# Spectral mixing behind a short convolution: Y brought into its second layout by TensorE transposes, the convolution taps loaded to one partition on another queue than the first x unit, and a reordered seam

## The chip, the cores and the metric

One core of one Trainium2 chip. The metric is the device time of one execution in microseconds (us); lower is better. The kernel before takes 183.05 us (median of 3 runs, 183.0 to 183.22). Ratios below are the mean time of one kernel's fast runs over that of the kernel before in the same rounds, so they are not quite the ratio of the medians that stand beside them. In the profile lines PE is TensorE's matmuls, PEld its weight loads, DVE VectorE, ACT ScalarE and POOL GpSimd; the granted clock is the share of its full clock that TensorE ran at. Instants in the text are us from the start of the span, which is 1.7 to 1.9 us shorter than the time in most executions.

## The reference, cut to what matters

```python
# x: (8, 3264, 192), weight: (8, 7)
w = softmax(weight)                       # taps, per head of 24 channels
x = causal 7-tap convolution of x with w  # along the sequence
X = rfft(x, axis=1)                       # only 64 modes are kept
Y[m] = X[m] @ (w_r[m] + 1j * w_i[m])      # 64 complex 192x192 matrices: 18.9 MB
y = irfft(Y, n=3264)
u = x + y
out = u + relu(u @ w_ch)                  # float32, 20 MB
```

## The kernel before

The kernel has a loading part (x, then the weights of the 64 modes in 16 groups, all through GpSimd's software queue, "the stream", cast to bf16 on the way), a seam from the last weights to the steady loop, and an output loop over 108 units. The parts that the change touches:

```python
# the start: taps broadcast to 128 partitions, then the first x unit, both on the sync queue
wraw = sp.tile([P, H, KK], F32, tag="wraw")
nc.sync.dma_start(out=wraw[:]..., in_=bass.AP(tensor=weight.tensor, ..., ap=[[0, P], [1, H * KK]]))
x32 = sp.tile([P, 8, D], F32, tag="x32")
nc.sync.dma_start(out=x32[:], in_=...)          # 1024 rows of 768 B
load_unit(0, 2)                                 # the software queue ("the stream") begins
...                                             # softmax of the taps on all 128 partitions

# two mode groups of the mix -> 128 rows of Y; a transfer makes the layout [mode rows, batch, channel]
def mix(g):
    ...
    nc.scalar.activation(out=ymix[:], in_=zt[:, 0:D], func=ACT.Copy, scale=...)
    nc.sync.dma_start(out=zy[16 * i:16 * i + 16, :, :], in_=ymix[:, :])   # 8 of these
def mix_t(g, ymix):                             # and the transposed copy yeT, by TensorE
    ...

# the seam, after the last weights
zw_part(0); zw_part(1)                          # 16 products yeT x w_ch into four banks, then copies
for n in range(4): gz(n)                        # four units were prefilled; gz = product with Z, relu
prefill(); gy(0); gz(4); gy(1); prefill(); gy(2); gz(5); gy(3)    # gy = product with Y, add, store
```

Of the kernel before, what the change touches and what calls it, by code (L numbers as in the profile page):

```python
# [9 lines left out]
ALU = mybir.AluOpType  # L10
ACT = mybir.ActivationFunctionType
AX = mybir.AxisListType
F32 = mybir.dt.float32
BF16 = mybir.dt.bfloat16
# [4 lines left out]
def kernel(  # L19
# [9 lines left out]
    nc = tc.nc  # L29
    B, S, D = x.shape  # L30
    H, KK = weight.shape
    MODES = moe_w_r.shape[0]
# [3 lines left out]
    P = 128  # L36
# [36 lines left out]
    def load_last():  # L73
# [8 lines left out]
    ident = constp.tile([P, P], BF16, tag="ident")  # L82
# [12 lines left out]

    setup_stack = ExitStack()
    sp = setup_stack.enter_context(tc.tile_pool(name="setup", bufs=1))
    wraw = sp.tile([P, H, KK], F32, tag="wraw")
    nc.sync.dma_start(out=wraw[:].rearrange("p h k -> p (h k)"),
                      in_=bass.AP(tensor=weight.tensor, offset=weight.offset, ap=[[0, P], [1, H * KK]]))  # L100

    x32 = sp.tile([P, 8, D], F32, tag="x32")
    nc.sync.dma_start(out=x32[:], in_=bass.AP(tensor=x.tensor, offset=x.offset + (WIN * 10 - OV) * D,
                                              ap=[[D, P], [WIN * D, 8], [1, D]]))
# [18 lines left out]
    win0 = constp.tile([P, D], BF16, tag="win0")  # L123
    win1 = constp.tile([P, D], BF16, tag="win1")
    wB0 = constp.tile([P, D], BF16, tag="wB0")
    for b in range(1, B):
# [9 lines left out]
        elif b == 4:  # L136
            nc.gpsimd.dma_start(out=wB0[0:64, :], in_=moe_w_ch[P:D, :])
            load_last()

    nc.vector.memset(cband[:], 0.0)  # L140

    NB = 32 + OV
# [2 lines left out]
    for g in range(4):  # L145
        i0 = OV if g == 0 else 0
        nc.vector.tensor_copy(out=diagc[32 * g:32 * g + 32, i0:NB],
                              in_=diag[32 * g:32 * g + 32, 32 * g - OV + i0:32 * g + 32])
    nc.vector.tensor_scalar(out=ident[:], in0=diag[:], scalar1=0.0, scalar2=None, op0=ALU.is_equal)

    halfpi = sp.tile([P, 1], F32, tag="halfpi")
# [4 lines left out]
    def make_k(u):  # L156
# [2 lines left out]
                                in0=sidx[:, w0:w0 + n].unsqueeze(2).to_broadcast([P, n, MODES]),  # L159
                                in1=midx[:, :].unsqueeze(1).to_broadcast([P, n, MODES]), op=ALU.mult)  # L160

    wmax = sp.tile([P, H], F32, tag="wmax")
    nc.vector.reduce_max(out=wmax[:], in_=wraw[:], axis=AX.X)
    wsub = sp.tile([P, H, KK], F32, tag="wsub")
    nc.vector.tensor_tensor(out=wsub[:], in0=wraw[:],
                            in1=wmax[:, :].unsqueeze(2).to_broadcast([P, H, KK]), op=ALU.subtract)
    wexp = sp.tile([P, H, KK], F32, tag="wexp")
    nc.scalar.activation(out=wexp[:], in_=wsub[:], func=ACT.Exp)
    nc.scalar.copy(out=x_all[:, 0, 10:18, :], in_=x32[:])
    wsum = sp.tile([P, H], F32, tag="wsum")  # L170
    nc.vector.reduce_sum(out=wsum[:], in_=wexp[:], axis=AX.X)
    nc.vector.tensor_scalar(out=wsum[:], in0=wsum[:], scalar1=1e-9, scalar2=None, op0=ALU.add)
    wrec = sp.tile([P, H], F32, tag="wrec")
    nc.vector.reciprocal(out=wrec[:], in_=wsum[:])
    wsb = sp.tile([P, H, KK], F32, tag="wsb")
    nc.vector.tensor_tensor(out=wsb[:], in0=wexp[:],
                            in1=wrec[:, :].unsqueeze(2).to_broadcast([P, H, KK]), op=ALU.mult)

    ps1 = ExitStack()
    pconv = ps1.enter_context(tc.tile_pool(name="pconv", bufs=3, space=PSUM))  # L180
    pxx = ps1.enter_context(tc.tile_pool(name="pxx", bufs=1, space=PSUM))



# [2 lines left out]
    for k in range(KK):  # L187
        nc.vector.scalar_tensor_tensor(out=scaled[:, k, :, :],
                                       in0=diagc[:, :].unsqueeze(1).to_broadcast([P, H, NB]), scalar=float(k),
                                       in1=wsb[:, :, k:k + 1].to_broadcast([P, H, NB]),  # L190
                                       op0=ALU.is_equal, op1=ALU.mult)
        for o in bps:
            nc.tensor.matmul(o[:, 0:H * NB], ident[:], scaled[:, k, :, :].rearrange("p h i -> p (h i)"),
                             start=(k == 0), stop=(k == KK - 1))
# [41 lines left out]
    yeT = constp.tile([P, 2, 2 * MODES * B], BF16, tag="yeT")  # L236
# [65 lines left out]
    dq = []  # L302
    xq = []

    nc.scalar.activation(out=wmax[:, 0:1], in_=halfpi[:], func=ACT.Sin)
    ascale = constp.tile([P, 1], F32, tag="ascale")

    zy = constp.tile([P, B, D], BF16, tag="zy")
# [54 lines left out]
    pt = ctx.enter_context(tc.tile_pool(name="pt", bufs=4, space=PSUM))  # L363
# [28 lines left out]
    for p in range(4):  # L392
        k = 0
        for i in range(11):
            n = 8 if i < 4 else 7
# [47 lines left out]


    mixed = [None]

    def mix(g):
        i, half = divmod(g, 2)
        if half == 0:
            mixed[0] = py.tile([P, 512], F32, tag="y", name="yp")  # L450
        zt = mixed[0]
        for j in range(3):
            for pos in range(4):
                nc.tensor.matmul(zt[32 * pos:32 * pos + 32, 0:D],  # L454
                                 xt[:, j, half:half + 2, :, MG * i + pos].rearrange("p s k -> p (s k)"),
                                 wtiles[g][:, pos, j, :], start=(half == 0 and j == 0),
                                 stop=(half == 1 and j == 2), tile_position=(0, 32 * pos),
                                 skip_group_check=True)
        if half == 0:
            return None  # L460

        ymix = workp.tile([P, D], BF16, tag="ymix")
        nc.scalar.activation(out=ymix[:], in_=zt[:, 0:D], func=ACT.Copy,  # L463
                             scale=ascale[:, 0:1] if i == 0 else 2.0 / S)
        nc.sync.dma_start(out=zy[16 * i:16 * i + 16, :, :], in_=ymix[:, :])
        return ymix

    def mix_t(g, ymix):
        zt = mixed[0]
# [9 lines left out]
    zwi = {}  # L479
    zwps = []  # L480

    def zw_part(h):
        for k in range(2):
            zp = zwps[2 * h + k]
            for i in range(2):
                b = 4 * h + 2 * k + i
                for e, wn in ((0, win0), (1, win1)):
                    nc.tensor.matmul(zp[:, D * i:D * i + D], yeT[:, e, b:2 * MODES * B:B], wn[:, :],  # L488
                                     start=(e == 0), stop=(e == 1), skip_group_check=True)
            zt = zwip.tile([P, 2 * D], BF16, tag=f"zw{h}{k}", name="zw")  # L490
            if h == 0:
                nc.vector.tensor_copy(out=zt[:, 0:D], in_=zp[:, 0:D])
                nc.scalar.copy(out=zt[:, D:2 * D], in_=zp[:, D:2 * D])
            else:
                nc.vector.tensor_copy(out=zt[:], in_=zp[:, 0:2 * D])
            b = 4 * h + 2 * k
            zwi[(h, 0, k)] = zt[:]
            zwi[(h, 1, k)] = zy[:, b:b + 2, :].rearrange("p b e -> p (b e)")

    def g_full(u, zp, part):  # L500
        h, w, k = u
# [39 lines left out]
    def relu(zp):  # L541
        return nc.scalar.activation(out=zp[:, 0:2 * D], in_=zp[:, 0:2 * D], func=ACT.Relu)  # L542
# [50 lines left out]

    ahead(0)
    gq = [0, 1]
    TPER = (1, 2, 1, 2, 2, 2, 1, 1, 2, 1, 2, 1, 2, 1, 1)
    zps = []

    def bank(n):
# [6 lines left out]
    def prefill():  # L606
        zps.append(bank(len(zps)))
        ab_full(seq[len(zps) - 1], zps[-1])
# [6 lines left out]
    for g in range(NGRP):  # L615
        last = g == NGRP - 1
        m = mix(g)
        if g == 6:
            wts0_stack.close()
            cTb = ctx.enter_context(tc.tile_pool(name="stashb", bufs=1)).tile([P, CTW], BF16, tag="cTb")  # L620
            nc.vector.memset(cTb[:, NSLOT * WIN:CTW], 0.0)
            cTs[3] = cTb[:, :]
        if g in (0, 1, 2):
            load_weights(g + 7, wp)
        elif 7 <= g and g + 4 < NGRP:
            load_weights(g + 4, None if g == 10 else wp)
        if not last:
            for _ in range(TPER[g]):
                t_next(2 if g < 6 else 3)
            if gq:  # L630
                g_part(gq.pop(0))
            if g == 2:
                load_weights(10, None)

            if g in (11, 13, 14):
                prefill()
        else:
            keep_warm(4)
        if m is not None:
            mix_t(g, m)  # L640
        if g == NGRP - 2:
            zwps += [pt.tile([P, 512], F32, tag="p", name="zwps") for _ in range(3)]
            prefill()
            keep_warm(6)
    zwps.append(py.tile([P, 512], F32, tag="y", name="zwps"))
# [7 lines left out]
    zwip = ctx.enter_context(tc.tile_pool(name="zwip", bufs=1, side="right"))  # L653


    def gz(n):
        g_full(seq[n], zps[n], 0)
        relu(zps[n])

    def gy(n):  # L660
        g_full(seq[n], zps[n], 1)
        finish_unit(seq[n], zps[n])

    zw_part(0)
    zw_part(1)
    for n in range(4):
        gz(n)
    prefill()
    gy(0)
    gz(4)  # L670
    gy(1)
    prefill()
    gy(2)
    gz(5)
    gy(3)
    N, NF = len(seq), 6
    zword, yword = {}, {}
    for j in range(NF, N + 6):
        o0, o1 = [], []
        if j < N:  # L680
            zps.append(bank(j))
            o0 = z_ops(seq[j], zps[j], 0)
        if NF <= j - 2 < N:
            o1 = z_ops(seq[j - 2], zps[j - 2], 1)
        zword[j] = run_pair(o0, o1, zword.get(j - 2))
        if NF <= j - 2 < N:
            relu(zps[j - 2])
        elif j - 2 < NF:
            gy(j - 2)
        o0, o1 = [], []  # L690
        if NF <= j - 4 < N:
            o0 = y_ops(seq[j - 4], zps[j - 4], 0)
        if NF <= j - 5 < N:
            o1 = y_ops(seq[j - 5], zps[j - 5], 1)
        yword[j - 4] = run_pair(o0, o1, yword.get(j - 5))
        if NF <= j - 5 < N:
            finish_unit(seq[j - 5], zps[j - 5])
# [29 lines left out]
```

## Time and profile before

| | before |
|---|---|
| time | 183.05 us |
| stream's first packets | 5.6 us |
| last mix (last weights landed) | 109.36 us |
| first half-height matmul with Y (the loop is under way) | 117.77 us |
| first of the last four adds (VectorE; start) | 174.68 us |
| end of the span | 181.4 us |

Read it as stretches: loading, which ends with the last mix; the seam, to the loop's first half-height Y matmul; and the loop. The lines themselves are shown in the prediction.

### The profile page before, as it was taken

The numbers are of one execution on the slowest core, as the hardware profiler recorded it, in microseconds if no ns is written. First come the engines' busy times: TensorE is split into PE (matmuls) and PEld (weight loads), VectorE is DVE, ScalarE is ACT, GpSimd is POOL, SyncE is SP. The second block draws the span as 40 slices with busy tenths as digits, with TensorE's granted clock in tenths as the row PEclk, the third lists the DMA queues.
The fourth block names the chain that finished last, engine by engine and source line by source line (L and its number), as shares of the span: only waits on it lengthen the run. The fifth ranks groups of instructions, "written<-read, shape, count | busy, mean of one in ns | idle before, by whom it ended". The sixth has DMA issues, their size and how long they took to land.

```text
span 181.4 us, 5402 instructions
## 1 busy us (share of the span) xinstructions
PE 147.8 (81%) x2115; PEld 128.9 (71%) x2115; DVE 127.8 (70%) x256; ACT 112.9 (62%) x189; POOL 48.8 (27%) x74
## 2 busy tenths in 40 slices
PE   0373579989889969894649977999999999999970
PEld 0242359978779959783538866699999999999940
DVE  5879986553544446974462554679999999999990
ACT  2353994555558617774444453588888888888850
POOL 7969332459322244432523100000000000000000
PEclk9999558999999999999985999999999999999997
DMA  2999999999999999999999990479999999999995
GB/s 60 247 191 191 192 192 191 193 190 192 193 192 193 204 206 207 206 208 210 203 206 207 207 178 11 150 238 306 345 358 353 349 324 366 348 341 328 326 353 188
DMA packets 66819, 42.37 MB, mean 234 GB/s; under 512 B 30218, under 2 KB 66794, under 8 KB 66794
## 3 DMA queue, kind: packets, MB, share of 16 engines
q0 software_dynamic: 36048, 19.75, 78.2%
q1 hardware_dynamic: 30746, 22.28, 37.5%
q8 instruction: 16, 0.26, 0.7%
q14 instruction: 9, 0.07, 0.1%
HBM read 40.31 MB, written 21.01 MB: 338 GB/s over the span
## 4 chain that ended last, share of the span: by engine, by line
DMA 54%; PE 38%; POOL 2%; issue 2%; DVE 1%; DVEq 0%; ACT 0%; POOLq 0%; ACTq 0%
DMA x_all<-in_x_dram 29%; PE z L520 19%; DMA wt<-in_moe_w_i_dram 19%; PE z L537 13%; DMA fst<-in_moe_w_i_dram 6%; PE tp L418 2%; POOL x_all L61 2%; PE z L502 1%; PE yp L454 1%; PE zwps L488 1%; DVE t L572 1%; PE z L510 0%; POOL wt L251 0%; DVEq L722 0%; ACT ymix L463 0%
## 5 line engine op out<-in xcount | busy, mean ns | idle before, releaser
L572 DVE TENSOR_TENSOR t<-z,x_all 128x384 f32<-128x384 f32 x108 | 59.4, 557 | 3.9 <-PE z L537 1.5
L542 ACT ACTIVATE z<-z 128x384 f32<-128x384 f32 x108 | 50.7, 476 | 11.6 <-PE z L520 1.7
L537 PE MATMUL z<-zy,gst 64*128 64x384 bf16 x204 | 46.1, 323 | 0.2
L520 PE MATMUL z<-zw,gst 64*128 64x384 bf16 x204 | 46.1, 323 | 0.0
L520 PE MATMUL z<-win,cTa 64*128 64x192 bf16 x375 | 40.9, 243 | 0.0
L267 ACT CAST x_all<-cp 122x864 bf16<-122x864 f32 (+2 forms) x34 | 28.7, 880 | 15.4 <-PE cp L260 15.2
L520 PEld LDWEIGHTS <-cTa 64*128 64x128 bf16 x450 | 34.9, 94 | 2.8
L260 PE MATMUL cp<-x_all,cband 128*128 128x192 bf16 (+2 forms) x192 | 25.9, 287 | 8.8 <-DVE x_all L269 4.6
L260 PEld LDWEIGHTS <-cband 128*128 128x128 bf16 x192 | 19.7, 109 | 12.7 <-issue 5.4
L61 POOL DMA_DIRECT2D x_all<-in_x_dram x23 | 22.0, 969 | 10.8 <-DMA x_all<-in_x_dram 8.5
L269 DVE CAST x_all<-cp 122x768 bf16<-122x768 f32 (+2 forms) x14 | 14.7, 1054 | 13.2 <-PE cp L260 13.2
L423 ACT COPY cTa<-tp 128x854 bf16<-128x854 bf16 (+1 forms) x16 | 14.1, 910 | 14.7 <-PE tp L418 14.7
L282 PE MATMUL xp<-x_all,fst 122*128 122x192 bf16 (+1 forms) x216 | 22.0, 251 | 0.9 <-DVE x_all L269 0.5
L282 PEld LDWEIGHTS <-fst 122*128 122x128 bf16 (+1 forms) x216 | 18.2, 99 | 2.1 <-DVE x_all L269 0.7
L520 PEld LDWEIGHTS <-gst 64*128 64x128 bf16 x204 | 18.9, 94 | 0.7 <-issue 0.7
L520 PE MATMUL z<-win,cTb 64*128 64x192 bf16 x135 | 19.2, 243 | 0.0
L422 DVE COPY cTa<-tp 128x854 bf16<-128x854 bf16 (+1 forms) x17 | 10.6, 623 | 10.8 <-PE tp L418 10.6
L520 PE MATMUL z<-wB,cTa 64*128 64x192 bf16 x75 | 18.2, 243 | 0.0
L537 PEld LDWEIGHTS <-gst 64*128 64x128 bf16 x204 | 16.1, 93 | 1.0 <-POOLq L554 0.9
L520 PEld LDWEIGHTS <-cTb 64*128 64x128 bf16 x162 | 14.4, 94 | 1.1
L418 PE MATMUL tp<-ident,x_all 122*128 122x122 bf16 x216 | 15.0, 228 | 0.0
L251 POOL DMA_DIRECT2D wt<-in_moe_w_r_dram x14 | 8.6, 612 | 20.2 <-PE yp L454 6.2
(98 smaller groups left out, 169.5 us busy)
## 6 DMA issues: line engine op xcount, KB each, us to landing
out_dram<-t SPq DMA_DIRECT2D x52, 384.0 KB, 4.1
wt<-in_moe_w_r_dram POOLq DMA_DIRECT2D x14, 288.0 KB, 11.4
wt<-in_moe_w_i_dram POOLq DMA_DIRECT2D x14, 288.0 KB, 11.6
x_all<-in_x_dram POOLq DMA_DIRECT2D x8, 432.0 KB, 12.3
x_all<-in_x_dram POOLq DMA_DIRECT2D x7, 480.0 KB, 13.0
x_all<-in_x_dram POOLq DMA_DIRECT2D x8, 384.0 KB, 14.4
x<-in_x_dram SPq DMA_DIRECT2D x1, 768.0 KB, 6.0
fst<-in_moe_w_r_dram POOLq DMA_DIRECT2D x2, 288.0 KB, 10.5
```

What stands on the lines that cost most here:

```text
L61: nc.gpsimd.dma_start(out=x_all[:, b, c0:c0 + n, :], in_=src)
L260: nc.tensor.matmul(cp[:, j, 0:GRP * n].rearrange("p (w e) -> p w e", w=n), cband[:, h, :], x_all[:, b, w0:w0 + n, GRP * h:GRP * h + GRP], ...
L267: nc.scalar.copy(out=dst, in_=srcv)
L269: nc.vector.tensor_copy(out=dst, in_=srcv)
L282: nc.tensor.matmul(xp[:, 0:D], fst[0:k, c, :], x_all[0:k, b, c, :], start=(u == FIRST[b] and c == w0), stop=(u == LAST[b] and c == w0 + n ...
L418: nc.tensor.transpose(tp[:, WIN * k:WIN * k + WIN], slot_lhsT(p, k0 + k), ident[0:WIN, 0:WIN])
L422: nc.vector.tensor_copy(out=got[0][0], in_=got[0][1])
L423: nc.scalar.copy(out=got[1][0], in_=got[1][1])
L520: return nc.tensor.matmul(o, lhsT, rhs, start=start, stop=stop, skip_group_check=True, tile_position=(lo, 0))
L537: return [lambda: nc.tensor.matmul(zp[:, 0:2 * D], gst[lo:hi, WIN * w:WIN * w + P], zwi[(h, 1, k)][lo:hi, :], start=False, stop=(r == 1), ...
L542: return nc.scalar.activation(out=zp[:, 0:2 * D], in_=zp[:, 0:2 * D], func=ACT.Relu)
L572: add = nc.vector.tensor_tensor(out=t[:, 2 * k:2 * k + 2, :], in0=zp[:, 0:2 * D].rearrange("p (i e) -> p i e", i=2), in1=x_all[:, 4 * h + ...
```

## The change

Its intent: take six of eight small transfers out of the full transfer engines by making the second layout of Y with TensorE from `yeT`, which is there anyway; take the 128-row tap load out of the way of the first x unit; and begin the output earlier with five units prefilled and products in separate banks. The core of the diff, with cuts:

```diff
-    wraw = sp.tile([P, H, KK], F32, tag="wraw")
-    nc.sync.dma_start(out=wraw[:]..., ap=[[0, P], [1, H * KK]]))
+    wraw = sp.tile([1, H, KK], F32, tag="wraw")
+    nc.scalar.dma_start(out=wraw[:]..., ap=[[H * KK, 1], [1, H * KK]]))
     ... softmax on one partition, then
+    nc.tensor.matmul(wps[:, 0, 0:H * KK], ones[:], wrow[:, :, :]..., start=True, stop=True)
+    nc.vector.tensor_copy(out=wsb[:], in_=wps[:, 0, 0:H * KK]...)
...
-        nc.sync.dma_start(out=zy[16 * i:16 * i + 16, :, :], in_=ymix[:, :])
+        if i >= YPE:                                                   # YPE = 6
+            nc.sync.dma_start(out=zy[16 * i:16 * i + 16, :, :], in_=ymix[:, :])
+    def y_back(half):                                                  # in groups 12 and 13
+        tp = pt.tile([P, 1024], BF16, tag="p", name="yb")
+        n = 16 * YPE
+        for i in range(4):
+            for e in range(2):
+                c0 = D * i + 64 * e
+                nc.tensor.transpose(tp[0:n, c0:c0 + P], yeT[:, e, 4 * half + i:n * B:B], ident[:])
+        nc.vector.tensor_copy(out=zy[0:n, 4 * half:4 * half + 4, :], in_=tp[0:n, 0:4 * D]...)
...
-    TPER = (1, 2, 1, 2, 2, 2, 1, 1, 2, 1, 2, 1, 2, 1, 1)   # pairs of x transposes per group
+    TPER = (1, 2, 1, 2, 2, 2, 1, 2, 2, 2, 2, 1, 1, 1, 0)
...
-    zw_part(0)
-    zw_part(1)
-    for n in range(4):
-        gz(n)
+    zw_mm(0, 0, zwps[0:2])
+    zw_mm(0, 1, zwps[2:3])
+    gz(0)
+    zw_mm(1, 0, zwps[0:1])
+    gz(1)
+    gz(2)
+    gy(0)
     ...
```

## The prediction

> **What bounds the kernel now.** I read the busy table and the 40 slices first, then the chain of waits in order of time, then the transfers by queue in narrow stretches, then the order of instructions around the seam between loading and output.
>
> The page says that no engine is full over the whole span, but that the transfer engines are full in slices 1 to 23, empty in slice 24, and then TensorE takes over:
>
> ```profile
> PE 147.8 (81%) x2115; PEld 128.9 (71%) x2115; DVE 127.8 (70%) x256; ACT 112.9 (62%) x189; POOL 48.8 (27%) x74
> ...
> PEclk9999558999999999999985999999999999999997
> DMA  2999999999999999999999990479999999999995
> DMA 54%; PE 38%; POOL 2%; issue 2%; DVE 1%; DVEq 0%; ACT 0%; POOLq 0%; ACTq 0%
> ```
>
> The chain of waits in order of time (start, length, what) gives the seam to 0.1 us:
>
> ```profile
> 99.78 9.54 DMA wt<-in_moe_w_i_dram
> 109.36 0.51 PE yp L454 x12
> 109.94 0.34 ACT ymix L463
> 110.72 0.30 DVE yeT L473
> 111.07 1.54 PE zwps L488 x16
> 115.03 0.51 PE z L520 x4
> 116.59 1.34 PE z L520 x21
> ```
>
> So the time has three parts: loading until the last weights land at 109.3; a seam of some 7.2 us (109.36 to the first iteration with both row tiles, about 116.5); then an output loop in which the chain consists of pieces of 0.33 and 0.25 us of TensorE, 0.5725 us per unit (118.09 to 173.05 is 96 iterations), to the end. In the loop VectorE's add takes 557 ns, so it is 97% as long; neither it nor ScalarE (476 ns) can make the loop shorter, and the change does not touch the loop. What can move is the instant at which the last weights land, and the seam.
>
> **Two measurements inside the loading part.** The queue counts (packets, MB, share of 16 engines) in stretches of 2 us, 73 to 75 and 75 to 77, without and with one of the small transfers that put Y into its second layout:
>
> ```profile
> q0 software_dynamic: 380, 0.41, 121.1%
> ...
> q0 software_dynamic: 337, 0.37, 106.5%
> q1 hardware_dynamic: 144, 0.05, 14.7%
> ```
>
> Clean stretches hold 379 to 383 packets of the load stream, stretches with a whole Y transfer 333 to 337. One Y transfer thus pushes out about 46 packets; at 190 packets per us it costs the load stream 46/190 = 0.24 us, although it is only 48 KB.
>
> The start, in stretches 1.8 to 3.4, 4.4 to 5.6, 5.6 to 6.6 and 6.8 to 7.8:
>
> ```profile
> q1 hardware_dynamic: 149, 0.05, 27.2%
> ...
> q1 hardware_dynamic: 569, 0.43, 109.1%
> ...
> q0 software_dynamic: 279, 0.11, 88.7%
> q1 hardware_dynamic: 217, 0.16, 49.1%
> ...
> q0 software_dynamic: 506, 0.19, 161.3%
> ```
>
> The load stream moves nothing before 5.6 us, though GpSimd has issued its first transfer by 2.4. Until 3.4 the engines spend their time at a 27% share on the taps (128 short packets, one per partition); the x unit, issued behind them on the same queue, then moves at full rate, and the stream comes in just as that unit goes out. This is the most important thing to see: the stream starts three microseconds after it was issued, and what stands ahead of it is the taps and the first x unit.
>
> **What the Trainium skill says.** "DMA: Bandwidth & Descriptors", section "Queues, rings and completion order": each of the 16 engines goes round robin between queue rows, but only at packet boundaries, and a packet may hold up to 64 descriptors. The x unit has 1024 rows, 64 per engine, so one engine could work it off without the stream getting a turn; in the trace the total stays at about 98 packets per 0.2 us from 5.4 to 6.4 while one queue replaces the other, which agrees with that and not with equal sharing. The same page, section "Specifications": a transfer below 512 B does not reach line rate; Y's rows are 384 B, and the 46 displaced packets of about 1.1 KB for 48 KB of Y agree. "TensorE: Matmul & The Clock Gate", Part 1: the clock falls to half after an idle window and comes back after a busy one; the trace shows granted clocks of 0.5 from 94 to 100 us, after a stretch (80 to 90) in which TensorE was 61% busy. "TensorEngine Tiling (Array Packing)", "Key Properties": changing the tiling mode drains TensorE; the seam shows waits of 0.16 to 0.17 us where full-height and half-height matmuls alternate.
>
> **The change part by part.**
>
> (1) Y by transposes. Six of the eight Y transfers go (the last two stay). All six lie in the full stream (issued from 71.4 to 99.5). 6 x 0.24 = 1.45 us earlier landing of the last weights. Added: 16 transposes, 16 x 0.07 = 1.2 us of TensorE, and two copies of 96x768 on VectorE, some 0.6 us each (the 128x854 copies take 0.60), in groups 12 and 13 of the mix. They must fit beside the stream: without Y a group of weights takes 544 packets / 190 = 2.86 us. Group 13 then has 0.48 of mix, 14 transposes (0.9), 8 new ones (0.6) and 0.3, so 2.3 us: it fits at full clock. Groups 7 to 10 get two pairs of transposes each: 0.5 + 1.8 + 0.3 = 2.6 to 2.9 us, tight but with lighter groups after them. Nothing of it comes onto the path.
>
> (2) Taps on one partition, x unit first. 128 short packets become one, on another queue, and the x unit is issued at 0.74 in place of 1.20. If its packets then start where the taps' did (1.8 to 2.4) and take the same 2.1 us per engine, it is done around 4.2 to 4.9 in place of 5.65 to 6.6. If the stream was only held up behind it, the stream starts 1.2 to 1.7 us earlier, and every later landing moves with it because the engines are full to the end. If the stream was not ready before 5.6 anyway, only the overlap is saved: from 5.6 to 6.6 it moved 279 of the 506 packets per us, so 0.45 us. I hold the first for about twice as likely and take 1.1 us. The taps' own path: the softmax waits for VectorE's set-up (4.6) more than for the taps (landed by 4.86), so the earlier landing wins 0.2; a broadcast matmul (0.25 with its latency), a copy (0.2) and two handovers (0.2) cost 0.65. The band matrix comes about 0.4 us later; conv is not on the chain, and TensorE makes up for it before 85 us, where it waits for weights again (gaps of 1.2 to 1.5 us per group). Off the path.
>
> (3) The seam. Before: mix to first product 1.7 us, 16 products 1.4, then six units with two late prefills, ready for the loop 7.2 us after the landing. After: the first product's two halves lie in two banks, so VectorE and ScalarE copy side by side: the first half-height copy can end about 0.4 us sooner, and the first relu starts 0.4 sooner (112.4 in place of 112.8, on the old clock). One prefill (0.33) leaves. But the order then runs product, relu, Y part unit by unit, each relu taking 0.44: the second waits for VectorE's 0.55 copy, the Y part of unit 1 for its relu (0.2 idle), the Y part of unit 5 for relu 5 at about 115.6, and unit 6 starts at about 115.1 on the old clock, which is 115.0 before. One mode change fewer saves 0.17. Sum: 0.1 us gained, uncertain by 0.4.
>
> Sum: 1.45 + 1.1 + 0.1 = 2.65 us. 183.05 - 2.65 = 180.4 us.
>
> **Rivals.**
>
> Rival A: the start gives nothing but 0.45, because the stream's first packet waits for descriptor generation on GpSimd. For it: no stream packet appears between 3.0 and 4.2 us, when the engines were far from full. Against: the exchange of one queue for the other with a constant sum. It would give 183.05 - 2.0 = 181.05.
>
> Rival B: TensorE becomes late at the end of the loading, so that the last weights land and find it busy, or the last load is issued too late. For it: two pairs of transposes in each of groups 7 to 10, and at half clock (as from 94 to 100 now, where 29 transposes took 3.1 us) a group would take over 4 us. Against: the last load is issued at 99.2 with about 8 us of loads still ahead of it, so that a microsecond of lateness starves nothing, and groups 11 to 14 are lighter than before. It would give back up to 1.5 us: about 182.
>
> Rival C: the clock. In the new order fewer transposes precede the seam, and if the half clock falls on 106 to 113 the seam costs 2 to 3 us more: 182.5 to 183.5. Against it: more transposes from 80 to 94 should keep TensorE busier exactly where it cooled off before, and the warm-up products remain.
>
> Rival D: the transfers removed were free, since the engines interleave. The count of displaced packets speaks against it; it would give 181.9.
>
> **Range and chances.** Centre 180.4. The start may add 0.6 or take away 0.65, the seam plus or minus 0.4, Y plus or minus 0.2; lateness or clock can cost 1 to 2. So 179.3 to 181.9 in 8 cases of 10. Over 2% faster means below 179.4: it needs both the full 1.7 at the start and a seam shorter by 0.5; 11%. Over 2% slower (above 186.7) would need the half clock for most of the seam and more: 2%. Within 2%: 87%.
>
> **What would show it.** In the changed profile the stream's first packet should come at 4 to 5 us (rival A: 5.3 or later). Between 72 and 104 the stream should hold about 190 packets per us throughout; groups should follow at 2.86 us rather than 2.98. The last mix should start at about 106.8 (109.36 before). From there to the first iteration with both row tiles should be 6.7 to 7.6 us, and the loop should keep 0.5725 us per unit. I am wrong if the last mix starts where it did, if TensorE's wait before the last mixes is gone, or if the granted clock is under 0.9 after the last landing.

## The result, and the profile after

The changed kernel took 180.52 us (median of 4 runs, 179.96 to 181.56) against 183.03 beside it (182.93 to 183.22): ratio 0.9868, 95% interval 0.9823 to 0.9914. That is the same within 2%, 2.5 us faster, and 0.1 from the forecast of 180.4.

The page of the changed kernel, the lines that answer to those shown before:

```profile
PE 147.8 (83%) x2132; PEld 129.4 (72%) x2132; DVE 128.0 (72%) x260; ACT 112.6 (63%) x188; POOL 48.8 (27%) x74
...
DMA  4999999999999999999999970669999999999996
PE 63%; DVE 16%; DMA 11%; issue 4%; POOL 1%; ACT 1%; DVEq 0%; POOLq 0%; ACTq 0%
```

The busy times hardly moved; the engines do the same work in a shorter span. The chain's shares look quite different (DMA 11% in place of 54%), but that is one link: in this execution TensorE came to the last mix a little after its weights, so the chain goes back along TensorE and not along the transfers. Two other executions of the same kernel, below, have the transfer back in that place. Shares of a chain between two engines that finish within a microsecond of each other say little. The chain in order of time at the seam:

```profile
103.87 0.72 PE yb L485 x4
...
105.90 1.10 PE z L532 x12
107.00 0.33 PE zwps L635 x6
107.33 0.43 PE yp L463 x12
107.84 0.34 ACT ymix L472
108.97 0.56 PE zwps L510 x4
113.02 0.51 PE z L542 x4
```

The last mix starts at 107.26 (the chain shows its end part), the loop's first half-height Y matmul at 115.55. Against before that is 2.1 and 2.2 us earlier. On the chain, four product matmuls now stand where sixteen stood. The first product with Z starts 0.96 us after the first of them (108.97 to 109.93), before 1.38 us (111.07 to 112.45).

The start, by queue (packets, MB, share of 16 engines), in stretches 1.8 to 2.8, 2.8 to 4.6, 4.6 to 5.2 and 5.2 to 6.2:

```profile
q1 hardware_dynamic: 64, 0.05, 50.4%
...
q1 hardware_dynamic: 791, 0.61, 101.8%
...
q1 hardware_dynamic: 184, 0.13, 70.3%
q0 software_dynamic: 111, 0.04, 58.7%
...
q0 software_dynamic: 504, 0.19, 160.6%
```

The x unit is now near its full rate from about 3.0 and gone by 5.2; the stream comes in at 4.8 and is at its full 504 packets per us from 5.2, where before it came in at 5.6 and was full at 6.7. By 8.0 us it has moved 1528 packets, before 984: at 505 per us that is 1.08 us.

In the stretch 73 to 75 the stream is as before between Y transfers, and now it stays so: from 72 to 104 each 2 us hold 365 to 384 packets, never 333.

```profile
q0 software_dynamic: 381, 0.41, 120.9%
```

### The profile page after: what moved, and what is told of

It reads as the page before. It is cut to its first block, busy times and chain, and to the rows that moved or that the text cites. A ratio compares the mean times of both kernels' runs of the same rounds, so it can differ in the third digit from the quotient of the medians.

```text
span 178.9 us, 5425 instructions
## 1 busy us (share of the span) xinstructions
PE 147.8 (83%) x2132; PEld 129.4 (72%) x2132; DVE 128.0 (72%) x260; ACT 112.6 (63%) x188; POOL 48.8 (27%) x74
## 4 chain that ended last, share of the span: by engine, by line
PE 63%; DVE 16%; DMA 11%; issue 4%; POOL 1%; ACT 1%; DVEq 0%; POOLq 0%; ACTq 0%
PE z L542 19%; PE z L559 14%; PE xp L290 8%; PE cp L268 8%; DMA wt<-in_moe_w_r_dram 6%; DMA wt<-in_moe_w_i_dram 5%; DVE x_all L277 5%; PE tp L426 4%; PE yp L463 2%; PE bps L201 2%; PE yb L485 2%; PE tp L302 1%; DVE kprod L223 1%; PE z L524 1%; DVE xs L294 1%
## 5 line engine op out<-in xcount | busy, mean ns | idle before, releaser
L268 PE MATMUL cp<-x_all,cband 128*128 128x192 bf16 (+2 forms) x192 | 24.8, 276 | 9.2 <-DVE x_all L277 3.9
L268 PEld LDWEIGHTS <-cband 128*128 128x128 bf16 x192 | 18.7, 105 | 13.0 <-issue 5.7
L426 PE MATMUL tp<-ident,x_all 122*128 122x122 bf16 x216 | 13.6, 217 | 0.0
```

Source lines behind the costliest of these rows:

```text
L268: nc.tensor.matmul(cp[:, j, 0:GRP * n].rearrange("p (w e) -> p w e", w=n), cband[:, h, :], x_all[:, b, w0:w0 + n, GRP * h:GRP * h + GRP], ...
L426: nc.tensor.transpose(tp[:, WIN * k:WIN * k + WIN], slot_lhsT(p, k0 + k), ident[0:WIN, 0:WIN])
```

## The experiments

Base: the changed kernel, run again twice. Landmarks of every profiled execution are gathered here; "packets" are those of the stream by 8.0 us, "Y" is the first half-height Y matmul, "adds" the start of the first of the last four adds.

| run | time | ratio | packets | last mix | Y | adds | end |
|---|---|---|---|---|---|---|---|
| before | 183.05 | | 984 | 109.36 | 117.77 | 174.68 | 181.4 |
| changed | 180.52 | 0.9868 | 1528 | 107.26 | 115.55 | 172.46 | 178.9 |
| e1 changed again | 180.39 | 0.9854 | 1508 | 107.15 | 115.44 | 172.35 | 178.6 |
| e11 changed, third | 180.46 | 0.9867 | 1531 | 106.85 | 115.14 | 172.05 | 178.4 |
| e2 old start | 181.24 | 0.9902 | 1001 | 108.00 | 116.29 | 173.20 | 179.4 |
| e3 no Y transposes | 182.60 | 0.9971 | 1486 | 108.67 | 118.07 | 174.98 | 181.6 |
| e4 old seam | 180.86 | 0.9863 | 1442 | 107.33 | 115.75 | 172.66 | 179.4 |
| e5 e3 and warm-up | 182.66 | 0.9983 | 1487 | 108.50 | 116.85 | 173.76 | 180.7 |
| e6 old taps behind x | 182.10 | 0.9930 | 814 | 108.50 | 116.80 | 173.71 | 180.2 |
| e7 new taps ahead of x | 181.18 | 0.9892 | 1314 | 107.54 | 115.84 | 172.75 | 178.8 |
| e8 x unit in the stream | 181.37 | 0.9911 | 1999 | 108.14 | 116.43 | 173.57 | 179.5 |
| e9 Y both ways | 182.26 | 0.9963 | 1501 | 108.38 | 116.66 | 173.57 | 180.4 |
| e10 seven Y by transposes | 180.85 | 0.9877 | 1497 | 107.16 | 115.47 | 172.60 | 178.9 |
| e12 e10 and warm-up | 181.19 | 0.9891 | 1518 | 106.80 | 115.12 | 172.27 | 179.6 |

Runs e1 to e4 were made together and share their runs of the kernel before (183.12), so did e5 to e8 (183.00) and e9 to e11 (183.00); e12 had 183.06 beside it. e1 to e4 and e9 to e11 have the same chip number; e5 to e8 and e12 ran on two others, where the changed kernel did not run, so they are compared with e1 and e11 across chips.

Two spreads to keep in mind. The last mix of the changed kernel itself starts between 106.85 and 107.26, so the difference of two single profiles there is good to about 0.4 us; the packets by 8.0 us are steadier, 1442 to 1531 (0.18 us) in the nine profiles with the changed start. And the time holds something that the profiled span does not: in some executions of e2, e4 and e6 to e9 (and in three of e1 and e11) time less span is 2.0 to 2.8 us. The medians of the recorded spans are therefore worth a look beside the times: 181.2 to 181.3 before; 178.6 and 178.7 in e1 and e11; 179.3 in e2, 180.85 in e3 and in e5, 178.6 in e4, 179.65 in e6, 178.95 in e7, 179.6 in e8, 180.3 in e9.

Theory: the two loading gains (Y out of the stream, the stream earlier) are added on the path because the last weights set the seam. Rivals: TensorE is late before the last mix and eats part; the stream at the start waits for its own descriptors, not for the hardware queue; the clock.

**e1, e11: the base.**

> The changed kernel once more, as the base of the comparisons. All theories: 180.5 us, single runs between 179.9 and 181.6, last mix at about 107.3 us in the trace with no transfer wait just before it.

> The changed kernel beside the two above on the same chip: 180.4, last mix at 107.2.

180.39 and 180.46 us. The last mix did wait here, which the profiled execution above did not show; TensorE's line of e1 for that group:

```profile
107.15 0.48 PE L463 MATMUL yp<-wt,xt 128*32 128x192 bf16 x12 [0.43 <-DMA wt<-in_moe_w_i_dram]
```

Idle 0.43 us until the transfer of the last weights: the loading still sets the seam. My expectation of "no wait" was taken from the one profile at half clock from 100 to 104 and was wrong for the common case.

**e2: old start.** The taps and softmax of the kernel before in the changed kernel:

```diff
-    wraw = sp.tile([1, H, KK], F32, tag="wraw")
-    nc.scalar.dma_start(out=wraw[:]..., ap=[[H * KK, 1], [1, H * KK]]))
+    wraw = sp.tile([P, H, KK], F32, tag="wraw")
+    nc.sync.dma_start(out=wraw[:]..., ap=[[0, P], [1, H * KK]]))      # ahead of the x unit
```

> The changed kernel with the old start (taps to 128 partitions ahead of the x unit, softmax on all partitions). Theory 1 (the parts add up, all on the path): stream starts at 5.6 us again, time 1.1 us more, 181.6. Theory 2 (the loading now ends before TensorE is ready, so part of the gain at the start is slack): the last mix waits for its weights again, and the time is only 0.2 to 0.6 more, 180.7 to 181.1.

181.24, 0.85 more than e1 (0.7 by spans); last mix 0.85 later; 507 packets fewer by 8 us, 1.0 us. Within the spread above, the stream's shift arrives whole at the last mix. Between the two theories, and nearer to the first: little is slack.

**e3, e5, e9: what the Y part is worth, and through what.** e3 sends all eight transfers and leaves out the transposes; e5 puts 16 plain matmuls into each of groups 12 and 13 where the transposes were; e9 keeps the transposes and sends the six transfers as well, into a spare tile:

```diff
# e3
-        if i >= YPE:
+        if True:
...
-            if g in (12, 13):
-                y_back(g - 12)
# e5: as e3, and
+            if g in (12, 13):
+                for _ in range(16):
+                    nc.tensor.matmul(warm[:, 0:P], ident[:], ident[:], start=True, stop=True)
# e9: as the changed kernel, and
+        else:
+            nc.sync.dma_start(out=spare[:, i % 2, :], in_=ymix[:, :])
```

> The changed kernel with all eight Y transfers and no Y transposes. Theory 1 (additive): 6 x 0.24 = 1.45 us more, 181.9 to 182.0. Theory 2 (the transposes themselves hold TensorE up before the last mix): the stream ends 1.45 later, but the last mix starts only some 0.6 to 0.9 later than in the changed kernel, 181.1 to 181.4, and it waits for its weights.

> All eight Y transfers, no Y transposes, but 16 plain warm-up matmuls in each of groups 12 and 13. The run without the Y transposes took 2.2 us more than the changed kernel, though its last weights came only 1.5 us later; its seam ran at half clock. Theory: the other 0.7 us is the clock, which the transposes had kept up. Then the clock is 1.00 from 106 to 118 us, the seam (last mix to first half-height Y matmul) is back at 8.3 us (9.4 without), and the time is 181.8 to 182.0. Rival: the 0.7 is the wait for Y's last transfers in the seam; then warm-up matmuls change nothing, 182.6.

> The changed kernel, transposes and all, with the six Y transfers added back into a tile that nobody reads: the same 128 rows of 384 B each, issued at the same places, while TensorE's work stays that of the changed kernel. Theory (the gain of the Y part is the room in the stream): the last mix starts 1.3 to 1.5 us later than in the changed kernel run beside it, time 1.4 more. Leaving Y's transposes out had cost 2.2 us: if the extra 0.8 is also due to the transfers (seam or drain of the output), it shows here, +2.2; if it is due to the missing TensorE work, it doesn't.

e3 took 182.60, 2.2 more than e1, where the theories had 1.45 and 0.6 to 0.9: both missed. Its last mix came 1.52 later, as six transfers at 0.24 each would have it. The rest of the profiled execution's lag stood in the seam (9.4 us in place of 8.3), and the granted clock says why; busy times by engine, then clock, transfer share and GB/s, from 108.67 to 110.5, to 114.0 and to 118.07:

```profile
108.67:110.50 1.83, 1.44 (x23) 0.99 (x24) 0.29 (x1) 0.33 (x1) 0.15 (x1) 1.00 0.00 0
110.50:114.00 3.50, 3.50 (x19) 2.45 (x20) 1.84 (x4) 1.75 (x5) 0.00 (x0) 0.53 0.06 14
114.00:118.07 4.07, 4.07 (x49) 2.94 (x47) 3.25 (x7) 1.87 (x5) 0.00 (x0) 0.98 0.53 175
```

Half clock in the middle of the seam. e5 was to prove that this is the whole of the extra 0.7. It did the first half of it: its clock is 1.00 throughout and its seam 8.35 us.

```profile
108.50:116.85 8.35, 7.79 (x87) 5.55 (x89) 5.20 (x11) 3.81 (x10) 0.14 (x1) 1.00 0.27 88
```

But the time did not follow: 182.66, no better than e3. The rival's number came (182.6), but not its reason, since the seam shows no wait for Y. In e5's profile the loop is only 1.4 later than e1's, and 0.7 is lost after the loop. So the clock explains e3's profiled execution and not the median; that theory falls as the explanation of the 2.2. e9, with TensorE's work as in the changed kernel, gives the transfers alone. Its last mix, and that of e11 beside it:

```profile
108.38 0.48 PE L464 MATMUL yp<-wt,xt 128*32 128x192 bf16 x12 [0.42 <-DMA wt<-in_moe_w_i_dram]
```

```profile
106.85 0.48 PE L463 MATMUL yp<-wt,xt 128*32 128x192 bf16 x12 [0.40 <-DMA wt<-in_moe_w_i_dram]
```

That is 1.53 later (1.1 to 1.2 against the other two profiles of the changed kernel), time 1.8 more (its interval is wide, 0.9919 to 1.0006), span 1.6 more. The room in the stream is thus the main thing, 1.1 to 1.6 us, and by spans it is the whole of e9. What the further 0.65 in the spans of e3 and e5 is stays open (see the drain below).

**e4: old seam.** The four-bank products, four prefilled units and order of the kernel before in the changed kernel:

```diff
-    zw_mm(0, 0, zwps[0:2])
     ...
+    zw_part(0)
+    zw_part(1)
+    for n in range(4):
+        gz(n)
     ...
```

> The changed kernel with the old seam (four banks of products first, four units prefilled at the landing, two later). My reading of the seam: worth 0.1, so 180.6 (within 0.3). Rival (the seam is what the change is about): 0.5 us or more, 181.0 or above; from the last mix to the first half-height Y matmul 8.4 us as before in place of 8.3.

180.86 against 180.39 by medians, 0.9863 against 0.9854 by ratios, so 0.2 to 0.5 us within intervals of about 0.25% each, and nothing by spans (178.6 in both). From last mix to Y 8.42 us, and 8.29 in e1 and e11: the seam is worth 0.13 us in the traces. The first relu of the changed kernel does start sooner, 3.03 us after the last mix (107.26 to 110.29) where it was 3.45 before; then the chain waits for a relu of 0.48 us (at 110.86), where the chain before stayed on TensorE, and most of the head start is used up.

**e6, e7, e8: what held the stream up at the start.** e6 has the old taps, issued behind the x unit; e7 the new one-partition taps on the sync queue ahead of the x unit; e8 loads the x unit through the stream, so no hardware transfer of any size is ahead of it:

```diff
# e6 (the softmax as in the kernel before, cut)
     nc.sync.dma_start(out=x32[:], in_=...)
+    nc.sync.dma_start(out=wraw[:]..., ap=[[0, P], [1, H * KK]]))
# e7
-    nc.scalar.dma_start(out=wraw[:]..., ap=[[H * KK, 1], [1, H * KK]]))
+    nc.sync.dma_start(out=wraw[:]..., ap=[[H * KK, 1], [1, H * KK]]))
# e8
-    nc.sync.dma_start(out=x32[:], in_=...)
+    load_win(0, 10, 8)
```

> The changed kernel with the old taps (128 short rows, softmax on all partitions), but issued behind the x unit on the same queue. If a transfer engine works off its hardware queue before it takes the stream, the 128 rows still come ahead of the stream: x unit done by 4.8, stream at full rate only at 5.5 to 6.2, time 0.5 to 0.9 more than the changed kernel's (181.0 to 181.3). Rival: only the order counts, not the rows: stream as in the changed kernel (about 1510 packets by 8 us), 180.4.

> The changed kernel with the one-partition taps issued on the sync queue ahead of the x unit. The x unit is issued some 0.4 us later, its packets are shifted by no more than that: 1300 to 1500 stream packets by 8 us, time 0 to 0.4 more than the changed kernel's. If the order were what counts, the stream would be back at 1000 packets by 8 us and the time at 181.2.

> The changed kernel with the first x unit loaded by the stream itself (cast on the way), so that no hardware transfer stands ahead of it. If the stream is ready at 3.4 and only held up by the hardware queue, its first packets come at about 3.4 us, and by 8 us it has moved some 2300 packets, 1024 of them the x unit: about 250 fewer of the rest than in the changed kernel, time 0.5 more or less equal. Rival (descriptor generation makes it late): first packets at 4.6 to 5.0 as in the changed kernel, so the x unit costs its whole 2.0 us, time 182.4.

e8 first, since it decides. The stream's packets from 3.0 to 4.0 us:

```profile
q0 software_dynamic: 64, 0.02, 43.0%
```

The stream's first packets come at 3.0, not at 4.6 or later: in the changed kernel it waits behind the x unit, and in the kernel before behind taps and x unit. The rival of slow descriptor generation is out. But 64 packets in a microsecond are few; the stream is at its full rate only from about 4.4, so what the x unit still holds up is the time from there to 5.2, not from 3.0. e8 is slower all the same (181.37; 1.0 more than e1, where I had 0.5 at most), since the x unit then costs the stream its 1024 packets: 975 others by 8 us against 1508, 533 fewer where I had 250.

e6 shows that the wait is not a sharing of the engines' time. In the stretch 5.2 to 6.2 and in 6.2 to 7.2, when the x unit is done and only the taps' short rows are left:

```profile
q0 software_dynamic: 56, 0.02, 22.8%
q1 hardware_dynamic: 54, 0.01, 4.6%
...
q0 software_dynamic: 358, 0.14, 114.9%
q1 hardware_dynamic: 26, 0.00, 2.0%
```

54 short packets, which take 4.6% of the engines' time, stand beside 56 stream packets in a microsecond that can hold 505. The two queues move nearly one packet for one, and together they fill 27% of the engines' time, where the full stream takes 160%: the stream loses time to waiting, not to the taps' transfer itself. Why a short row holds it up so long is not shown. Here, at the start, the stream is full only once the hardware queue is empty. Its 814 packets by 8 us are 694 fewer than e1's, 1.37 us, and the last mix is 1.35 later than e1's; the time is 1.7 more, the span 1.05. I had expected 0.5 to 0.9: the stream waits as expected, the price of 128 short rows is larger. e7, one short row ahead on the same queue, costs 194 packets, 0.38 us, the delay of the x unit's issue, as expected; its last mix is 0.39 later than e1's. Its time was not as expected: 0.8 more, where I had 0 to 0.4, and equal to the rival's 181.2. The packets (1314, not the rival's 1000) and the spans (0.35 more) speak for the theory; the other 0.4 lies outside the span. So 128 rows that became one are worth 313 packets, 0.62 us (e2 against e7), and keeping that row from delaying the x unit another 0.4.

**e10, e12: a version that might beat both.** Seven of eight Y parts by transposes, all 128 columns of `yeT` as weights, after the mix's own transpose in group 13 and in group 14; both drop six warm-up matmuls in group 14; e12 adds 6 and 12 in groups 11 and 12:

```diff
-    YPE = 6
+    YPE = 7
+    nc.gpsimd.memset(yeT[:, :, P * YPE:], 0.0)
...
-                nc.tensor.transpose(tp[0:n, c0:c0 + P], yeT[:, e, 4 * half + i:n * B:B], ident[:])
+                nc.tensor.transpose(tp[:, c0:c0 + P], yeT[:, e, 4 * half + i:2 * MODES * B:B], ident[:])
```

> A version meant to beat both: seven of eight Y parts by transposes, taken over all 128 columns in place of 96, after the mix's own transpose in group 13 and in group 14 in place of warm-up products. Theory 1 (a weight load of 96 columns is the slow kind: 8 transposes took 1.57 us where the product's 8 loads of 128 columns took 0.7): 8 transposes take 0.7 to 0.8 us; one more transfer leaves the stream's last two microseconds, so the last mix starts 0.2 to 0.4 us earlier, time 0.3 less than the changed kernel beside it. Theory 2 (the stride of 16 B makes them slow): 1.5 to 2 us each, TensorE is late before the last mix, time 0.5 to 1 more.

> The version with seven Y parts by full-width transposes, with 6 and 12 plain warm-up matmuls in groups 11 and 12. Without them TensorE ran at half clock from 103.6 to 107 in the profiled run and began the last mix at 107.16 without waiting, though the stream had ended by 106.4. Theory: with the clock at 1.00 the last mix waits for its weights again and starts at 106.4 to 106.7; ratio to before 0.984 (the changed kernel had 0.985 to 0.987). Rival: the last weights' landing, not the clock, sets it: 107.1, ratio as the changed kernel's.

The transposes did become quick: TensorE's line for eight of them in e11 (96 columns) and in e12 (128 columns), both at full clock:

```profile
102.13 1.57 PE L485 MATMUL yb<-ident,yeT 128*96 128x128 bf16 x8
```

```profile
104.81 0.66 PE L486 MATMUL yb<-ident,yeT 128*128 128x128 bf16 x8
```

But neither version is faster than the changed kernel: 180.85 and 181.19, with ratios 0.9877 and 0.9891. In e10 TensorE fell to half clock from 103.3 to 106.7 and was late at the last mix. In e12 it was not: clock 1.00, the last mix waits 0.67 for its weights again. It starts at 106.80, though, the same as e11's 106.85. The stream's last packet ends at 106.41 in e10 and 106.43 in e12, against 106.43, 106.76 and 106.46 in the three profiles of the changed kernel. So no gain from one transfer fewer shows at the last weights. The rival of that expectation is the nearer, though e12's ratio is above the changed kernel's.

**The drain.** e12 also shows where single executions differ: its last four adds begin at 172.27, 0.2 after e11's, and its span ends 1.2 later. When the last four adds begin, 2100 to 2360 output packets are still to be moved in every one of the fourteen profiles, at the queue's full rate for most of the time. The kernel before, from 175 to 177:

```profile
q1 hardware_dynamic: 997, 0.74, 109.3%
```

At 499 packets per us the rest takes 4.4 us, and a last landing follows; from the start of the last four adds to the end is 5.9 to 7.4 us over the profiles, without order by what was changed (6.7 before; 6.2 to 6.4 in the three profiles of the changed kernel; 6.7 to 6.9 in e3, e5 and e9; 7.4 in e12). From the end of the very last add it is 4.0 to 5.4 us. e12's trace explains its own excess in part: the last three store issues on SyncE took 3.1 us where e11's took 2.3, and the output queue ran nearly dry, 94 packets from 174.9 to 175.4 where the full rate gives 250. The 0.5 us or so in e3, e5 and e9 I cannot attribute.

## Why the prediction was right

The forecast was 180.4 us, the time 180.52. Each term was measured by itself, and the mechanism was the one forecast; that the two numbers meet within 0.1 us is in part luck.

1. *The bound* (last weights, then seam, then a loop at TensorE's pace) held. In all fourteen profiles the first half-height Y matmul and the first of the last four adds are 56.9 to 57.2 us apart. In e1 the groups of weights follow each other at 2.86 us (84.04 to 101.22 for six), as forecast. One statement was too simple: I called the loop TensorE's "to the end" and did not see the 4.4 us of output that wait when the last four adds begin. And one of the signs named for being wrong, no wait before the last mix, did show in the first profiled execution; e1 and e11 show the wait.
2. *Y transfers, 1.45 us.* e9 put them back with TensorE's work unchanged: 1.1 to 1.5 at the last mix, 1.6 in the span, 1.8 in the time. The count of displaced packets sized them well; rival D (free, since interleaved) is refuted. One reading in the prediction does not hold: the 46 displaced packets do not show a loss for short rows, since at 1.1 KB each they held 50 KB, about the transfer's own 48 KB. e3 and e5 lost 2.2 without the transposes, and some 0.65 of it is not settled.
3. *The start, 1.1 us.* Stream earlier by 1.08 us; e2 lost 0.85 without it. Rival A fell with e8. That the middle value fitted is luck: it averaged two outcomes, 1.2 to 1.7 and 0.45, and neither came. The x unit took until 5.2 and not until 4.2 to 4.9 (its first microsecond, 1.8 to 2.8, moved only 64 packets). The stream was held up by it, but would not have been at full rate before 4.4 either (e8). The band matrix, forecast 0.4 later, came 0.2 earlier (first convolution at 12.04, before 12.24), so nothing of it came onto the path.
4. *The seam, 0.1 us.* 0.12 between the profiles of before and after, 0.13 in e4's, too little to see in the times. The first relu's head start, forecast at 0.4, was 0.42.
5. *TensorE beside the stream.* Here a size was wrong: 8 new transposes were to take 0.6 us and took 1.57 at full clock. Group 13 still fitted, so nothing came onto the path in e1 and e11; in the first profiled execution, at half clock from 100 to 104, the last mix came with no wait, 0.83 us after the stream's last packet (0.39 in e1 and e11), which is rival B to the degree of 0.4 us.
6. *The clock*, rival C, did not strike the changed kernel's seam in its three profiles (1.00 from 104 to 114 in each), but it did in e3.

The sum by experiment depends on the yardstick: 1.6 + 0.7 + 0 = 2.3 us by spans (e9, e2, e4), 1.8 + 0.85 + 0.47 = 3.1 by times. Forecast 2.65; measured 2.5 in time and 2.5 to 2.7 in span. The parts add up to the whole within about 0.6 us and no better.

## What to carry to other kernels

When one queue is full from start to end, count what it moves in stretches with and without a neighbour: displaced packets divided by the queue's rate price a small transfer, and here that price is about what its removal brought. Bytes gave the same price only at the stream's own rate (48 KB at 0.41 MB in 2 us is 0.24 us); at the 370 GB/s of the output's stores they would have given 0.13. Look at what stands ahead of a long stream at its first instant: 128 broadcast rows of 224 B held up everything behind them, and one row with a TensorE broadcast did the same job. Don't read a theory off the chain's shares of one execution when two engines finish within a microsecond of each other; a second profile may show the other one.

## What the Trainium skill lacked or had wrong

- "DMA: Bandwidth & Descriptors", "Queues, rings and completion order", has the engines go round robin between queues at packet boundaries. The wait behind the x unit fits that, as the prediction argued: no stream packet before 4.8 us, though without the x unit the first came at 3.0 (e8). What the page does not lead one to expect is e6, where the two queues' counts are near one for one and the engines still stood mostly unused: 56 stream packets of 505 possible in a microsecond beside 54 short ones. In the full stream later, a Y transfer displaced 46 packets and no more.
- No page has the price of a broadcast load: 128 rows of 224 B, all from the same place in memory, cost the stream 1.37 us when issued behind the x unit (e6).
- "DMA: Bandwidth & Descriptors", "Specifications", says that transfers under 512 B miss line rate. That does not show here: 48 KB in 128 rows of 384 B between parts of SBUF cost 0.24 us of a full stream whose packets in that time held as many bytes, and six cost 1.1 to 1.5 (e9).
- "TensorE: Matmul & The Clock Gate", "Weight-path perf modes — Fast Weight Load (FWL) and DoubleRow", says that fast loads are on when there are 128 weights. The trace agrees, and gives the price of missing it: a transpose with 96 columns as weights took 196 ns (1.57 us for 8, e11), one with 128 columns 83 ns (0.66 for 8, e12), though it makes a third more rows.
- No page gives a trn2 rate for stores in 768 B rows: 499 packets per us, 370 GB/s, in the drain.
